# A gated H3 layer with its gradients on one core: VectorE dependence delay in the FFT stage's order, key halves loaded before the weights, D taps before the shift taps

## The chip, the cores and the metric

The kernel runs on one core of one Trainium2 chip. The metric is device time in microseconds (us) of one execution; before the change the median of six runs is 519.81 us (518.73 to 521.49). Engines are named as the profile names them: PE is the matmul engine (PEld its weight loads), DVE is VectorE, ACT is ScalarE, POOL is GpSimd, SP is SyncE, which issues DMAs.

## The reference

The forward function, with S = 2048 rows, D = 512 channels, F = 1376 and everything in bf16, is

```python
xn = layernorm(q)                                   # no scale, no offset
k_shift = sum over t of k shifted by t rows * shift_k[:, t]     # 4 taps
kv = k_shift * v
y = irfft(rfft(kv, 2S) * rfft(ssm_k, 2S))[:S] + kv * ssm_D      # along S
s = xn * y
h = sigmoid(xn @ w_gate) * (xn @ w_up)
g = silu(h @ w_down)
out = q + s * g
```

The kernel returns `out` and, for a given `grad_out`, the gradients with respect to q, k, v, shift_k, ssm_k, ssm_D, w_gate, w_up and w_down (ten outputs).

## The kernel before

**Stages.** The work has three stages on the same core. The FFT stage (to about 148 us) computes the long convolution with FFTs written as matmuls, and beside it the gate/up products of nine of the 16 row tiles (`f_gen`). The middle stage (`stepB`, to about 343 us) does the gate's output product, its gradient and the row gradient, tile by tile. The last stage runs the convolution backwards (`frontC`, `backC`) beside the weight gradients (`dW`).

**The FFT stage.** Channels go in four groups of 128 (`cg` 0 to 3). Four generators give the work; `run_streams` interleaves them:

- `strK` transforms the kernel taps of a group: `k_t` adds the D tap to tap 0 on DVE and transposes on PE, `step1` multiplies by the cosine and sine table `Cf`, `flip` transposes, `step3` multiplies by a block-diagonal matrix. Each result is stored (`KK_d`, POOL's queue), and its halves are swapped into a second tile `Ks` by two DMAs on SP's queue.
- `strV` forms k_shift * v for a group on DVE: four multiplies by a tap row of `skb`, three adds, and a multiply by v, each 128x2048. `step1` follows.
- `strX` does `flip` and `step3` for that product, multiplies it by the two tap tiles on DVE (the second product needs `Ks`), and returns through `inv3` and `inv1`.
- `f_gen` has 32, 32 and 24 128x128 matmuls for one row tile (parts 0, 1 and 2, `pi`), a sigmoid on ACT and a multiply on DVE for each; `f_ln` is the row tile's layer norm on DVE and POOL, `f_xt` its transposes.

Every PE result lies in PSUM and is copied out ("evicted") by `evac`, which may run on either ACT or DVE.

**What sets the order.** Instructions aren't issued as they are written. `Rec` records all of them with their dependences, and `Rec.order` (a greedy list scheduler) gives each engine one fixed list. It keeps a clock for each engine (`free`) and an estimate of when each operation's inputs are there (`ready`), and always takes the operation that can start first. Two of its rules are touched here. Between `late` and `early` (operation numbers) a dependent operation on the same DVE or ACT is counted as ready at its predecessor's end plus 0.034 us and a ready one within 0.125 us may be taken in front of it; outside of these numbers it is counted as ready as soon as the engine is free. `late` was set at the end of the FFT stage (operation 2406), `early` at the start of the last (5157). The other rule is the choice between ACT and DVE for an eviction: an eviction of a bf16 result (a transpose) has `bias` 0.3, and DVE takes it as if it were ready 0.3 us sooner.

An engine runs its list strictly in this order; a DMA queue's issues too. The DMAs of the start are written in this order: on ACT's queue the shift taps `skr` and the D taps `Dcol_b`; on SP's queue the SSM taps of group 0 (`ld_KT`), two row tiles, the first 512 columns of both gate weights (`ld_w(0, 512)`), the key and value columns of group 0 (`ld_k(0)` with its two halo pieces, `ld_v(0)`), a row tile, and the other weights. A key or value group is 512 KB in pieces of 256 bytes. The shift taps are spread over the partitions by four 1-row matmuls, whose results ACT copies into `skb`.

Of the kernel before, what the change touches and what calls it, by code (L numbers as in the profile page):

```python
# [16 lines left out]
P = 128  # L17
# [25 lines left out]
class Arena:  # L43


    def __init__(self, slab, nbytes):
        self.slab = slab
        self.holes = [(0, nbytes)]
# [44 lines left out]
class Ring:  # L93
# [9 lines left out]
    def next(self):  # L103
        a = self.aps[self.i % len(self.aps)]
        self.i += 1
        return a
# [64 lines left out]
class Rec:  # L171
# [8 lines left out]
    def __init__(self, nc, tc, slab, psum):  # L180
        self.nc, self.tc, self.psum = nc, tc, psum
        self.slab_name = slab.name
        self.ops = []
        self.lastw, self.readers = {}, {}
        self.late, self.early = 1 << 30, 1 << 30
        self.cache = {}
        for e in self.ENGS:
            setattr(self, e, EngRec(self, e))
# [161 lines left out]
    def order(self):  # L350
# [21 lines left out]
        free = {e: 0.0 for e in self.ENGS}  # L372
        soon = {e: [] for e in self.ENGS}
        now = {e: [] for e in self.ENGS}
        either = []
# [30 lines left out]
        while ndone < len(ops):  # L406
            best = None
            for e in self.ENGS:
                near = 0.125 if e in ("vector", "scalar") and self.late <= lo < self.early else 0.0
                while soon[e] and soon[e][0][0] <= free[e] + near:  # L410
                    heapq.heappush(now[e], heapq.heappop(soon[e])[1])
                c = None
                if now[e]:
                    n0 = now[e][0]
                    if near and ops[n0].ready > free[e]:
                        n0 = min((n for n in now[e] if ops[n].ready <= free[e] and n < n0 + 60), default=n0)
                    c = (max(free[e], ops[n0].ready) if near else free[e], n0, e, 0)
                elif soon[e]:
                    c = (soon[e][0][0], soon[e][0][1], e, 0)
                if either and e in ("scalar", "vector"):  # L420
                    o = min(either, key=lambda o: (max(o.ready, free[e]) - (o.bias if e == "vector" else 0.0), o.n))
                    s = (max(o.ready, free[e]), o.n, e, 1)
                    late = free["scalar"] - s[0] + o.bias
                    if e == "scalar" or late > (0.4 if c is None or c[0] > s[0] + 0.6 else 1.6):
                        if c is None or s[:2] < c[:2]:
                            c = s
                if c is not None and (best is None or c[:2] < best[:2]):
                    best = c
            if best is None:
                raise RuntimeError("the order is stuck: " + str({k: len(v) for k, v in blocked.items()}))  # L430
            t, n, e, shared = best
# [24 lines left out]
            d = 0.0  # L456
            if op.dma:
                occ, d = self.dcost(alt)
                me, other = ("gpsimd", "hw") if e == "gpsimd" else ("hw", "gpsimd")
                t = max(t, pipe[me] - 12.0)  # L460
# [20 lines left out]
            while held and held[0] <= lo + LOOK:  # L481
                o = ops[heapq.heappop(held)]
# [15 lines left out]
            for s in op.succ:  # L498
                if s < 0:
                    o = ops[~s]  # L500
# [4 lines left out]
                o = ops[s]  # L505
# [131 lines left out]
def kernel_impl(ctx, tc, A_q, A_k, A_v, A_shift_k, A_ssm_k, A_ssm_D, B_x, B_w_gate, B_w_up, B_w_down,  # L637
                grad_out, out_0, out_1, out_2, out_3, out_4, out_5, out_6, out_7, out_8, out_9):
    nc = tc.nc
# [21 lines left out]
    def ps_acc(shape, dt=f32, name=None):  # L661
        return nc.ps("acc", shape, dt)
# [8 lines left out]
    skb = Ring(ar, [4, D]).ap  # L671
    Dcol_b = Ring(ar, [NG]).ap
# [29 lines left out]
    def f_ln(i, part=None):  # L702
        xj = T[i]["xq"]
        if part == 1:
            f_ln2(i)
            return
        st = T[i]["st"] = lnst.next()
        nc.vector.bn_stats(st[:, 0:6], xj)
        nc.vector.bn_aggr(st[:, 6:8], st[:, 0:6])
        nc.vector.tensor_scalar_add(st[:, 8:9], st[:, 7:8], LN_EPS)  # L710
        nc.gpsimd.tensor_tensor(out=rstd_all[:, i:i + 1], in0=st[:, 8:9], in1=neghalf, op=ALU.pow)
        if part is None:
            f_ln2(i)

    def f_ln2(i):
        xj, st = T[i]["xq"], T[i]["st"]
        if PS["wide"]:
            nc.vector.tensor_scalar(xnA[:, i, :], xj, st[:, 6:7], rstd_all[:, i:i + 1], ALU.subtract, ALU.mult)
            return
        nc.vector.scalar_tensor_tensor(nmr_all[:, i:i + 1], st[:, 6:7], -1.0, rstd_all[:, i:i + 1], ALU.mult, ALU.mult)  # L720
        nc.scalar.activation(xnA[:, i, :], xj, ACT.Identity, bias=nmr_all[:, i:i + 1], scale=rstd_all[:, i:i + 1])

    def f_xt(i):
        if POS[i] > 3 and not 8 < POS[i] < 12:
            T[i]["xnT"] = xnT_r.next()
            nc.sync.dma_start_transpose(T[i]["xnT"], xnA[:, i, :])
            return
        pt = ps_tr([4, 128], name="ps_xnT")
        for db in range(4):
            nc.tensor.transpose(pt[:, db, :], xnA[:, i, db * 128:(db + 1) * 128], ident)  # L730
        T[i]["xnT"] = xnT_r.next()
        nc.evac(T[i]["xnT"], pt[:], 512)
# [65 lines left out]
    def ld_KT(cg):  # L798
        stA["KT", cg] = KT_r.next()
        nc.sync.dma_start(stA["KT", cg], A_ssm_k[cg * GW:(cg + 1) * GW, :])  # L800
# [5 lines left out]
    def ld_k(cp):  # L806
        c0, c1 = cp * GW, (cp + 1) * GW
        kh = kh_r.next()
        nc.gpsimd.memset(kh[0:1, 0:3, :], 0.0)
        nc.sync.dma_start(kh[:, 3:, :], kC[:, :, c0:c1])  # L810
        ld_halo(nc.sync, kh[:, 0:3, :], kHalo[:, 0:3, c0:c1])
        stA["kh", cp] = kh

    def ld_v(cp):
        vg = vg_r.next()
        nc.sync.dma_start(vg, vC[:, :, cp * GW:(cp + 1) * GW])
        stA["vg", cp] = vg
# [3 lines left out]
    skr, ones1 = skr_r.ap[0:1, :], ones_r.ap[0:1, :]  # L821
    def ld_x(i):
        T[i]["xq"] = xq_r.next()
        nc.sync.dma_start(T[i]["xq"], qC[:, i, :])
    nc.scalar.dma_start(skr, A_shift_k.rearrange("(o d) t -> o (d t)", o=1))
    nc.scalar.dma_start(Dcol_b, A_ssm_D.rearrange("(cg p) -> p cg", p=P))
    ld_KT(0)
    ld_x(SEQ[0])
    ld_x(SEQ[1])

    def ld_w(f0, f1):
        for w, src in ((wg, B_w_gate), (wu, B_w_up)):
            nc.sync.dma_start(w[:, :, f0:f1], src[:, f0:f1].rearrange("(db p) f -> p db f", p=P))
    ld_w(0, 512)
    ld_k(0)
    ld_v(0)
    ld_x(SEQ[2])
    ld_w(512, 1024)
    ld_w(1024, F)
# [22 lines left out]
        pass  # L862
    next(consts)
    f_ln(SEQ[0])
    next(consts)
    f_xt(SEQ[0])
    f_ln(SEQ[1])
    next(consts)
    for db in range(4):
        pb = ps_acc([512])  # L870
        nc.tensor.matmul(pb[:], ones1, skr[:, db * 512:(db + 1) * 512], start=True, stop=True)
        nc.scalar.copy(skb[:, :, db * 128:(db + 1) * 128], pb[:].rearrange("p (d t) -> p t d", t=4))
    ld_KT(1)
    ld_k(1)
    ld_v(1)
# [197 lines left out]
    for r in (KT_r, KC_r, kh_r, vg_r, acc_r, term_r, kvt_r, QgK_r, QgV_r, QfK_r, QfV_r, KF_r, Ks_r, Bg_r, Xc_r, P1_r, Ci_r):  # L1073
        r.free()
    PS["mm"], PS["wide"] = "mm1", False
    nc.late = len(nc.ops)


    zw = {k: Ring(ar, [D], at=kv_off["kh"] + 1024 * q) for q, k in enumerate(("sigz", "gate", "s_out", "dgate", "t2"))}
# [404 lines left out]
@with_exitstack  # L1484
def kernel(
    ctx: ExitStack,
    tc: tile.TileContext,
    A_q: bass.AP,
    A_k: bass.AP,
    A_v: bass.AP,  # L1490
    A_shift_k: bass.AP,
    A_ssm_k: bass.AP,
    A_ssm_D: bass.AP,
    B_x: bass.AP,
    B_w_gate: bass.AP,
    B_w_up: bass.AP,
    B_w_down: bass.AP,
    grad_out: bass.AP,
    out_0: bass.AP,
    out_1: bass.AP,  # L1500
    out_2: bass.AP,
    out_3: bass.AP,
    out_4: bass.AP,
    out_5: bass.AP,
    out_6: bass.AP,
    out_7: bass.AP,
    out_8: bass.AP,
    out_9: bass.AP,
):
    kernel_impl(tc, A_q, A_k, A_v, A_shift_k, A_ssm_k, A_ssm_D, B_x, B_w_gate, B_w_up, B_w_down,  # L1510
                grad_out, out_0, out_1, out_2, out_3, out_4, out_5, out_6, out_7, out_8, out_9)
# [30 lines left out]
```

## Time and profile before

| | us |
| --- | --- |
| median of six runs | 519.81 |
| the profiled execution | 518.73 |
| its span | 516.9 |
| PE busy | 490.1 |
| DVE busy | 390.5 |
| ACT busy | 351.2 |
| POOL busy | 126.4 |

Lines such as "L522" stand for one helper through which every operation is issued, so line numbers don't tell operations apart; shapes and places in time do. In answers about a window, "(x)" behind a busy time is the number of instructions. In a timeline the columns are start, duration, engine, operation, output and inputs, number, and the idle time in front with what ended it. The busy time of an operation can overlap the one behind it on the same engine, since an engine starts the next before the last one has ended. "ACTq" and "SPq" are the issues of DMAs on these engines.

### The profile page before, as it was taken

How to read it: one execution, taken by the hardware profiler on the slowest of the kernel's cores; microseconds unless marked ns; L12 is line 12 of the kernel's file. 1: busy time of each engine (PE TensorE's matmuls, PEld its weight loads, DVE VectorE, ACT ScalarE, POOL GpSimd, SP SyncE). 2: the span in 40 equal slices, each digit the busy share in tenths (PEclk: the TensorE clock that was granted, in tenths of full speed). 3: DMA queues.
4: the chain of work that ended last, by engine and by line, in shares of the span. 5: the costliest groups of instructions: out<-in, count | busy, mean ns of one | idle time of the engine just before them, and what ended most of it. 6: DMA issues, size and time to landing. Idle time of an engine off the chain costs nothing.

```text
span 516.9 us, 13489 instructions
## 1 busy us (share of the span) xinstructions
PE 490.1 (95%) x5381; PEld 350.7 (68%) x5437; DVE 390.5 (76%) x771; ACT 351.2 (68%) x468; POOL 126.4 (24%) x243
## 2 busy tenths in 40 slices
PE   4899898899999999999999999999999999999997
PEld 3788697798986676666666556644676755775744
DVE  8789999777848789867779988427658678883754
ACT  7799999889974564465545546426879968776621
POOL 7344433455503423414153311000000000000000
PEclk9999999999999999999999999999999999999999
DMA  8999985689999555737399947899798699999984
GB/s 223 296 291 316 294 271 180 216 248 257 233 201 228 154 162 155 216 105 192 119 250 241 267 148 179 209 277 234 168 268 222 188 264 221 244 206 254 202 224 120
DMA packets 181705, 112.93 MB, mean 218 GB/s; under 512 B 131433, under 2 KB 166153, under 8 KB 181386
## 3 DMA queue, kind: packets, MB, share of 16 engines
q1 hardware_dynamic: 170008, 78.17, 62.9%
q0 software_dynamic: 11104, 33.89, 20.4%
q8 instruction: 42, 0.69, 0.5%
q14 instruction: 21, 0.17, 0.1%
q10 hardware_dynamic: 530, 0.01, 0.1%
HBM read 37.65 MB, written 45.72 MB: 161 GB/s over the span
## 4 chain that ended last, share of the span: by engine, by line
PE 73%; ACT 10%; DVE 7%; issue 4%; DMA 3%; POOL 2%; SPq 0%; ACTq 0%; DVEq 0%; POOLq 0%
PE psum L522 73%; ACT slab L522 10%; DVE slab L522 7%; DMA out_dram<-slab 1%; POOL slab L522 1%; DMA slab<-in_A_ssm_D_dram 1%; DMA slab<-in_grad_out_dram 0%; POOL hF_d L522 0%; POOL KK_d L522 0%; SPq L522 0%; ACTq L522 0%; POOL out_dram L522 0%; POOL sF_d L522 0%; DVEq L522 0%; POOLq L522 0%
## 5 line engine op out<-in xcount | busy, mean ns | idle before, releaser
L522 PE MATMUL psum<-slab 128*128 128x128 bf16 (+5 forms) x5381 | 490.1, 253 | 23.6 <-ACT slab L522 11.1
L522 PEld LDWEIGHTS <-slab 128*128 128x128 bf16 (+2 forms) x5437 | 350.7, 99 | 162.7 <-issue 19.1
L522 DVE TENSOR_TENSOR slab<-slab 128x512 bf16<-128x512 bf16 (+6 forms) x488 | 268.6, 600 | 50.1 <-ACT slab L522 34.3
L522 ACT CAST slab<-psum 128x1024 bf16<-128x1024 f32 (+5 forms) x272 | 219.5, 852 | 93.2 <-PE psum L522 76.8
L522 ACT ACTIVATE slab<-psum 128x512 bf16<-128x512 f32 (+2 forms) x80 | 54.0, 679 | 39.3 <-PE psum L522 36.0
L522 ACT ACTIVATE slab<-slab 128x512 bf16<-128x512 bf16 (+3 forms) x71 | 56.8, 810 | 15.0 <-DVE slab L522 14.1
L522 ACT COPY slab<-psum 128x1024 bf16<-128x1024 bf16 (+1 forms) x43 | 38.3, 936 | 13.8 <-PE psum L522 13.6
L522 POOL DMA_DIRECT2D out_dram<-slab x32 | 17.5, 547 | 93.9 <-DVE slab L522 93.9
L522 DVE TENSOR_TENSOR slab<-psum,slab 128x512 bf16<-128x512 f32 (+2 forms) x47 | 29.3, 626 | 14.3 <-ACT slab L522 11.1
L522 DVE CAST slab<-psum 128x1024 bf16<-128x1024 f32 (+2 forms) x22 | 24.6, 1116 | 15.3 <-PE psum L522 13.1
L522 POOL MEMSET slab<- 1x384 bf16 (+2 forms) x13 | 4.8, 376 | 116.7 <-PE psum L522 116.4
L522 POOL DMA_DIRECT2D hF_d<-slab x48 | 26.1, 546 | 23.5 <-DVE slab L522 22.5
L522 DVE SCALAR_TENSOR_TENSOR slab<-psum,slab 128x512 bf16<-128x512 f32 x16 | 11.0, 689 | 27.1 <-PE psum L522 27.1
L522 POOL DMA_DIRECT2D KK_d<-slab x32 | 17.5, 547 | 27.3 <-ACT slab L522 20.1
L522 POOL DMA_DIRECT2D slab<-in_A_q_dram x29 | 16.1, 555 | 16.5 <-DMA out_dram<-slab 5.2
L522 DVE SCALAR_TENSOR_TENSOR slab<-slab 128x512 bf16<-128x512 bf16 (+3 forms) x41 | 17.1, 417 | 0.9
L522 DVE STREAM_TRANSPOSE slab<-slab 128x1024 f32<-128x1024 f32 x8 | 14.3, 1826 | 2.7 <-ACT slab L522 2.7
L522 DVE TENSOR_SCALAR slab<-slab 128x1 f32<-128x1 f32 (+9 forms) x48 | 12.1, 268 | 4.6 <-POOL slab L522 3.7
L522 POOL TENSOR_TENSOR slab<-slab 128x1 f32<-128x1 f32 x16 | 11.2, 701 | 16.6 <-DVE slab L522 16.4
L522 POOL DMA_DIRECT2D slab<-hF_d x18 | 9.7, 542 | 12.5 <-PE psum L522 10.1
L522 DVE BATCH_NORM_STATS2 slab<-slab 128x6 f32<-128x512 bf16 x16 | 10.9, 684 | 0.0
L522 DVE COPY slab<-psum 128x1024 bf16<-128x1024 bf16 (+1 forms) x14 | 9.0, 648 | 2.3 <-ACT slab L522 1.7
(20 smaller groups left out, 36.3 us busy)
## 6 DMA issues: line engine op xcount, KB each, us to landing
KK_d<-slab POOLq DMA_DIRECT2D x32, 256.0 KB, 4.7
slab<-KK_d SPq DMA_DIRECT2D x16, 512.0 KB, 4.5
slab<-in_A_k_dram SPq DMA_DIRECT2D x8, 512.0 KB, 8.3
hF_d<-slab POOLq DMA_DIRECT2D x32, 128.0 KB, 4.3
slab<-slab SPq DMA_DIRECT2D x32, 128.0 KB, 5.1
out_dram<-slab POOLq DMA_DIRECT2D x32, 128.0 KB, 3.0
uF_d<-slab SPq DMA_DIRECT2D x32, 128.0 KB, 2.6
gF_d<-slab SPq DMA_DIRECT2D x32, 128.0 KB, 2.8
```

Source lines behind the costliest of these rows:

```text
L522: getattr(getattr(self.nc, eng), meth)(*[place(v) for v in a], **{x: place(v) for x, v in k.items()})
```

## The change

Six edits. `late` is 0, so the dependence delay of DVE and ACT operations and the 0.125 us look-ahead also hold in the FFT stage. The bias of a bf16 eviction is now added on ACT as well as taken off on DVE, so ACT prefers another eviction that is ready within 0.3 us. `Dcol_b` is loaded in front of `skr`. Key and value of group 0 are loaded in front of the first weight columns. The four matmuls and copies that make `skb` are recorded earlier. The line that set `late` at the stage's end is gone.

```diff
@@ class Rec, __init__ @@
-        self.late, self.early = 1 << 30, 1 << 30
+        self.late, self.early = 0, 1 << 30
@@ order @@
                 if either and e in ("scalar", "vector"):
-                    o = min(either, key=lambda o: (max(o.ready, free[e]) - (o.bias if e == "vector" else 0.0), o.n))
+                    sg = 1.0 if e == "scalar" else -1.0
+                    o = min(either, key=lambda o: (max(o.ready, free[e]) + sg * o.bias, o.n))
                     s = (max(o.ready, free[e]), o.n, e, 1)
@@ kernel_impl @@
+    nc.scalar.dma_start(Dcol_b, A_ssm_D.rearrange("(cg p) -> p cg", p=P))
     nc.scalar.dma_start(skr, A_shift_k.rearrange("(o d) t -> o (d t)", o=1))
-    nc.scalar.dma_start(Dcol_b, A_ssm_D.rearrange("(cg p) -> p cg", p=P))
     ld_KT(0)
     ld_x(SEQ[0])
     ld_x(SEQ[1])
...
-    ld_w(0, 512)
     ld_k(0)
     ld_v(0)
+    ld_w(0, 512)
     ld_x(SEQ[2])
...
     f_ln(SEQ[0])
+    for db in range(4):
+        pb = ps_acc([512])
+        nc.tensor.matmul(pb[:], ones1, skr[:, db * 512:(db + 1) * 512], start=True, stop=True)
+        nc.scalar.copy(skb[:, :, db * 128:(db + 1) * 128], pb[:].rearrange("p (d t) -> p t d", t=4))
     next(consts)
     f_xt(SEQ[0])
     f_ln(SEQ[1])
     next(consts)
-    for db in range(4):
-        pb = ps_acc([512])
-        nc.tensor.matmul(pb[:], ones1, skr[:, db * 512:(db + 1) * 512], start=True, stop=True)
-        nc.scalar.copy(skb[:, :, db * 128:(db + 1) * 128], pb[:].rearrange("p (d t) -> p t d", t=4))
     ld_KT(1)
...
-    nc.late = len(nc.ops)
```

## The prediction

> **What bounds the kernel now.** I read the busy tenths first, then busy time by stretches, then what PE waited for, then single timelines. Columns of the stretches: PE, PEld, DVE, ACT, POOL busy, granted clock, DMA share, GB/s.
>
> ```profile
> PE   4899898899999999999999999999999999999997
> DVE  8789999777848789867779988427658678883754
> ACT  7799999889974564465545546426879968776621
> ...
> 0.00:22.00 22.00, 13.08 (x118) 10.58 (x119) 18.79 (x62) 17.45 (x24) 10.64 (x27) 1.00 0.99 262
> 22.00:36.00 14.00, 13.15 (x205) 11.94 (x205) 10.56 (x14) 11.71 (x16) 7.69 (x15) 1.00 0.94 263
> 36.00:50.00 14.00, 12.48 (x201) 11.45 (x200) 13.79 (x18) 13.85 (x17) 5.18 (x10) 1.00 1.06 333
> 50.00:64.00 14.00, 12.08 (x169) 10.07 (x168) 13.90 (x22) 13.77 (x17) 6.66 (x13) 1.00 0.99 284
> 64.00:78.00 14.00, 13.46 (x221) 12.51 (x219) 13.25 (x18) 13.31 (x17) 4.39 (x8) 1.00 0.89 277
> 78.00:94.00 16.00, 12.87 (x179) 10.63 (x179) 14.43 (x21) 16.00 (x19) 6.38 (x11) 1.00 0.43 143
> 94.00:148.50 54.50, 53.47 (x857) 49.77 (x865) 38.58 (x67) 47.85 (x60) 25.62 (x49) 1.00 0.97 253
> 148.50:300.00 151.50, 150.77 (x1510) 102.64 (x1523) 123.87 (x331) 82.00 (x139) 53.83 (x101) 1.00 0.72 187
> ```
>
> Before 22 us everything is start-up. From 36 to 94 us ACT never rests (56.93 of 58), DVE almost never, and PE loses 7.1. From 94 us on PE is full: it loses 1.0 to 148.5 and 0.7 to 300. So PE idle before 94 us is what there is to win: 8.0 in 22 to 94 (14.00 - 13.15 and so on), 8.9 at the start.
>
> ```profile
> PE psum L522 <- ACT slab L522: 5.6, 17, 0.5
> PE psum L522 <- DVE slab L522: 3.6, 5, 1.5
> ```
>
> PE's waits from 20 to 100 us: ACT's evictions, seventeen times, none over 0.5, so a rate and no single wait.
>
> Both kernels' instruction lists, side by side, bound the change in time. PE's are the same from its 1,948th weight load (148.5 us), and so are DVE's, ACT's, POOL's and SP's from 142 to 147 us. As PE is full from there, a shift at 148.5 us goes through to the end, and nothing else can change.
>
> **The change part by part**
>
> **Dependent DVE operations.**
>
> ```profile
> 2.30 0.43 DVE L522 TENSOR_SCALAR slab<-slab 128x512 int32<-128x512 int32 x1
> 2.76 0.69 DVE L522 SCALAR_TENSOR_TENSOR slab<-slab 128x512 int32<-128x512 int32 x1
> 3.37 0.69 DVE L522 TENSOR_TENSOR slab<-slab 128x512 int32<-128x512 int32 x1
> 4.09 0.43 DVE L522 TENSOR_SCALAR slab<-slab 128x512 int32<-128x512 int32 x1
> ```
>
> The second reads the first and starts 0.03 after its end; the third is independent and starts 0.08 before the second ends. A neighbouring dependent pair costs 0.117. In the FFT stage such pairs fall from 58 to 36: 22 x 0.117 = 2.6 of DVE. 17 of the 22 lie before 16 us, in the making of the tables, and I count them at nothing: after the second table multiply DVE now comes 0.5 early to the D taps' add and waits for that load (which landed at 5.9; 0.5 sooner by its earlier place on ACT's queue), and each of the first two layer norms now waits for POOL's power (0.68 and 1.01) with too little in between, some 0.5 and 0.8. So the last table's sine stays near 16.1. The other five give 0.6 on DVE, beside ACT: nothing.
>
> The Trainium skill, VectorE: DVE Perf Modes, section Rules for kernel authors, speaks against this part: for chained operations the drain happens regardless, so count operations. By that the reordering would give 0 instead of 2.6 of DVE time. The rows above show 0.117 between the two kinds, so I go by the rows; it doesn't alter the sum, which uses neither.
>
> **Evictions (bias and delay together).** Durations from 20 to 100 us:
>
> ```profile
> L522 ACT CAST slab<-psum 128x1024 bf16<-128x1024 f32 x47 | 46.2, 1102 | 3.5 <-PE psum L522 3.2 <-issue 0.2
> L522 ACT COPY slab<-psum 128x1024 bf16<-128x1024 bf16 x24 | 24.3, 1063 | 2.1 <-PE psum L522 1.9
> L522 DVE CAST slab<-psum 128x1024 bf16<-128x1024 f32 x4 | 4.9, 1220 | 0.6 <-PE psum L522 0.6
> L522 DVE COPY slab<-psum 128x1024 bf16<-128x1024 bf16 x6 | 4.0, 684 | 0.2 <-PE psum L522 0.2
> ```
>
> Less the overlap, the steps on ACT are 0.905 for either type, on DVE 1.15 (f32) and 0.60 (bf16). In front of the last eviction of group 0's inverse transform (at 71.95), six large evictions leave ACT and three large and one small (0.5) come: 6 x 0.905 - 3 x 0.905 - 0.5 = 2.2 less. At group 1's `inv3` (90.6) it is 3.4 less, at its inverse transform (101.8) 2.2, over the whole stage 15 large and 3 small against 13 and 1: 2.8. DVE gets nine bf16 and six f32 and gives four and nine: about +0.2 in all, +1.5 by 72 us.
>
> **The start.** I followed ACT's new list with these steps. The four copies into `skb` (0.5 each, none added) come earlier, before the third sine pair, with no reader before 26 us. Group 0's tap transposes go in front of the second sine pair and ACT waits for them about 1.2; all four `step1` evictions now come before the first row tile's transposes are evicted, so that tile's first matmuls start at about 19 instead of 13.5-14.4. That is paid back: before, PE had two matmuls of the second row tile in front and stood 1.5 at 20-21.4 for a DVE eviction at 20.96; now it runs through. `flip` 0 comes off PE at about 23.2 (22.8 before), and the first Ci eviction starts on ACT at about 37.0 (36.4 before) with 1.4 more work done. Taken as 0; ends -0.7 and +1.0.
>
> **Key halves first.** The first weight columns were complete at 8.9, the 256-byte key and value packets ran from 8.2 to 14.1. Swapped, the weights are complete at about 8.9 + 5.9 = 14.8. What hides this is the late first row tile (19); without it 14.8 against 13.5, 1.3 lost. On SP's queue everything to the other weights keeps its sum. The small halo piece moves ahead of group 1's key load, whose own halo piece stood long on SP (timeline; minimum/median/maximum of such issues in ns):
>
> ```profile
> 16.23 7.88 SPq L522 DMA_DIRECT2D slab<-in_A_k_dram  x3
> ...
> L522 SPq DMA_DIRECT2D slab<-in_A_k_dram x11: 527/688/6715, 3.2 to 54.4; - x11
> ```
>
> Three key issues in 7.88: the load, its halo piece (6.715, the longest of the eleven) and only then, at 23.6, the small one. It goes out by 17 instead of 23.6 and lands (4.4 later, the median of such pieces) by 22 instead of 28. DVE's eight shift operations of group 0 (9.9, from 28.53) can then start at 26.3, behind the first tile's last product, and end near 36.7 instead of 38.4 with one gate product (0.6) among them. Group 0's four `step1` evictions, first at 40.9 on ACT, then start at about 37.9. This lengthens nothing ACT-bound, but keeps ACT fed while it has less to do: 0 by itself.
>
> The Trainium skill, DMA: Bandwidth & Descriptors, the table at its head, asks for at least 512 B per transfer for line rate, which speaks against putting 256-byte pieces first. The rows have 1 MB of them in 5.9 and 1 MB of 1024-byte weight packets in 3.9 (5.0 to 8.9). It sets which load is late, and the start hides that.
>
> **Key group 2 on SP.** In the new list this 512 KB load is issued in front of two swaps of `Ks`. A transfer behind it stood 5.36 (37.94), one behind the value load 4.64 (44.61). Swap 0 then lands near 45.6, needed at 48; swap 1 near 51.6, needed near 52. Counted 0; ends 0 and +4.6.
>
> **POOL.** Its queue issues the same DMAs (0.54 each) in another order; the power operations keep their place among loads. 0; up to 0.5 either way.
>
> **Sum.** ACT has 2.2 less in front of group 0's end and again of group 1's, 2.8 in the stage, and was the bound from 36 to 94. I take 2.4, between the two. Far ends: 0 (in-order waits take all), and 3.4 + 1.9 = 5.3, as at group 1's `inv3` PE is 34 matmuls further (x 0.056). 518.73 - 2.4 = 516.3 for the profiled execution, which is 1.1 below its median; so 517.4.
>
> **Rivals**
>
> - *More: PE is full earlier.* If ACT's 3.4 and PE's 1.9 both hold at 90 us, PE runs full from there: 3.5 to 5.3 off, 514.5 to 516.3 (median). For: PE loses 3.1 in 78-94. Against: DVE has 3 to 4 of shift work put off there and must still do it.
> - *No change: ACT waits in order.* A gate sigmoid stands eleven places earlier on ACT (from 67.3 to about 57), one of `inv3`'s evictions is on DVE behind two products. Five such waits of 0.5 (the largest ACT wait above) cost 2.4: 519.8. Against: PE is up to three PSUM slots ahead.
> - *Slower: swap 1 of `Ks` late.* If it lands after 54.2, over 2.2 after its need, the DVE product waits, behind it two more, and ACT stands at `inv3` 1. At 4.6 late the net is +2.2: 522.0. For: DMA share is 0.99 to 1.06 there. Against: margin 0.4, and POOL's stores don't grow.
> - *The delay rule changes nothing:* excluded, 22 pairs go.
>
> **How the numbers follow.** Forecast 0.45 (own range 516.3 to 518.2), more 0.17, no change 0.21, slower 0.17. 0.3% is 1.6 us, about what a measurement of this kernel can tell from no change: under 518.2 is faster, over 521.4 slower. Faster 0.45 + 0.17 = 0.62, same 0.21; slower 0.17, with the start's +1.0 on top of an ACT wait in it. The range runs from 514.6, near the far end of "more", to 521.5: some 0.04 below, 0.16 above.
>
> **What would show it.** After: DVE's shift operations of group 0 start near 26.3; PE idle in 22 to 94 falls from 8.0 to about 5.6; ACT is still full in 36 to 90 and its busy time is about 2.8 lower; the last sine of the tables stays near 16; the later stages keep their lengths. It is wrong if DVE's products of group 0 wait for swaps, if ACT waits over 1 us at once between 36 and 94, or if the start moves by more than 1.

## The result and the profile after

| | before | after |
| --- | --- | --- |
| median, us | 520.04 (38 runs, 518.56 to 523.95) | 517.54 (17 runs, 516.21 to 519.86) |
| profiled execution, its span | 518.73, 516.9 | 519.86, 518.1 |
| ACT busy | 351.2 | 348.1 |
| DVE busy | 390.5 | 389.9 |
| PE busy | 490.1 | 490.5 |

The ratio is 0.9951 (95% interval 0.9938 to 0.9964): 2.5 us faster. One thing is needed to read the profile: the profiled execution of after is the longest of its 17, that of before the second shortest of its 38, so their spans stand the wrong way round. Places inside the execution can still be compared. Lines L522 became L523, since the change adds a line above the helper.

Busy time by stretches, after; columns as in the prediction (length, then PE, PEld, DVE, ACT, POOL busy, granted clock, DMA share, GB/s):

```profile
0.00:22.00 22.00, 11.54 (x88) 8.90 (x89) 17.55 (x61) 17.23 (x24) 11.70 (x29) 1.00 1.00 265
22.00:36.00 14.00, 13.87 (x204) 12.91 (x205) 10.52 (x13) 10.23 (x14) 5.36 (x11) 1.00 0.88 222
36.00:50.00 14.00, 12.34 (x201) 11.41 (x200) 12.20 (x17) 13.79 (x17) 5.07 (x10) 1.00 1.03 305
50.00:64.00 14.00, 13.79 (x207) 12.20 (x208) 13.89 (x23) 14.00 (x19) 7.25 (x14) 1.00 0.97 292
64.00:78.00 14.00, 13.78 (x230) 13.09 (x231) 13.22 (x15) 13.71 (x17) 4.39 (x9) 1.00 1.05 305
78.00:94.00 16.00, 15.01 (x225) 13.00 (x225) 15.40 (x27) 15.05 (x20) 7.59 (x13) 1.00 0.69 226
94.00:148.50 54.50, 52.89 (x821) 48.30 (x829) 40.07 (x71) 47.96 (x59) 24.12 (x47) 1.00 0.99 231
```

PE idle from 22 to 94 us fell from 8.0 to 3.2 (14.00 - 13.87, and so on): the gain. PE idle before 22 us rose from 8.9 to 10.5: a loss. What PE waited for from 20 to 100 us (total, times, longest) says the same, 2.9 in place of 9.2:

```profile
PE psum L523 <- ACT slab L523: 2.3, 5, 0.7
PE psum L523 <- DVE slab L523: 0.6, 2, 0.4
```

Evictions from 20 to 100 us (engine, operation, count, busy and mean ns):

```profile
L523 ACT CAST slab<-psum 128x1024 bf16<-128x1024 f32 x50 | 49.0, 1103 | 1.8 <-PE psum L523 1.8
L523 ACT COPY slab<-psum 128x1024 bf16<-128x1024 bf16 x20 | 21.0, 1073 | 1.0 <-PE psum L523 1.0
L523 DVE COPY slab<-psum 128x1024 bf16<-128x1024 bf16 x10 | 6.6, 683 | 0.0
L523 DVE CAST slab<-psum 128x1024 bf16<-128x1024 f32 x2 | 2.4, 1224 | 0.7 <-PE psum L523 0.7
```

DVE took four more of the bf16 results, which cost it 0.68 each, and gave two of the f32 ones, which cost it 1.22, back to ACT: 70 of 82 are on ACT, where it was 71 of 81. What counts for the theory is their place: up to the end of group 0's inverse transform the list has 49 large ones on ACT in place of 52.

### The profile page after: what moved, and what is told of

Same layout as the page of the kernel before. It is cut to its first block, busy times and chain, and to the rows that moved or that the text cites. A ratio compares the mean times of both kernels' runs of the same rounds, so it can differ in the third digit from the quotient of the medians.

```text
span 518.1 us, 13487 instructions
## 1 busy us (share of the span) xinstructions
PE 490.5 (95%) x5377; PEld 351.7 (68%) x5437; DVE 389.9 (75%) x775; ACT 348.1 (67%) x464; POOL 125.3 (24%) x243
## 4 chain that ended last, share of the span: by engine, by line
PE 70%; ACT 12%; DVE 10%; issue 4%; DMA 4%; SPq 0%; POOL 0%; DVEq 0%; ACTq 0%; POOLq 0%
PE psum L523 70%; ACT slab L523 12%; DVE slab L523 10%; DMA out_dram<-slab 1%; DMA slab<-in_A_ssm_D_dram 1%; DMA slab<-KK_d 1%; DMA slab<-in_grad_out_dram 0%; DMA hF_d<-slab 0%; SPq L523 0%; POOL out_dram L523 0%; DVEq L523 0%; ACTq L523 0%; POOLq L523 0%
## 5 line engine op out<-in xcount | busy, mean ns | idle before, releaser
L523 PE MATMUL psum<-slab 128*128 128x128 bf16 (+3 forms) x5377 | 490.5, 254 | 23.6 <-ACT slab L523 10.0
L523 PEld LDWEIGHTS <-slab 128*128 128x128 bf16 (+1 forms) x5437 | 351.7, 99 | 162.0 <-DVE slab L523 15.7
L523 DVE TENSOR_TENSOR slab<-slab 128x512 bf16<-128x512 bf16 (+6 forms) x488 | 268.2, 600 | 53.8 <-ACT slab L523 34.4
L523 ACT CAST slab<-psum 128x1024 bf16<-128x1024 f32 (+3 forms) x275 | 222.4, 854 | 93.0 <-PE psum L523 79.7
L523 ACT ACTIVATE slab<-psum 128x512 bf16<-128x512 f32 (+2 forms) x80 | 53.8, 679 | 45.8 <-PE psum L523 42.6
L523 ACT ACTIVATE slab<-slab 128x512 bf16<-128x512 bf16 (+3 forms) x71 | 56.5, 809 | 14.7 <-DVE slab L523 14.0
L523 ACT COPY slab<-psum 128x1024 bf16<-128x1024 bf16 (+1 forms) x36 | 33.1, 948 | 11.2 <-PE psum L523 11.2
L523 POOL DMA_DIRECT2D out_dram<-slab x32 | 17.5, 547 | 93.3 <-DVE slab L523 93.3
L523 DVE TENSOR_TENSOR slab<-psum,slab 128x512 bf16<-128x512 f32 (+2 forms) x47 | 29.2, 625 | 11.0 <-ACT slab L523 8.5
L523 POOL DMA_DIRECT2D hF_d<-slab x48 | 26.1, 546 | 37.6 <-DVE slab L523 33.3
L523 POOL MEMSET slab<- 1x384 bf16 (+2 forms) x13 | 4.5, 352 | 122.5 <-PE psum L523 119.1
L523 DVE SCALAR_TENSOR_TENSOR slab<-psum,slab 128x512 bf16<-128x512 f32 x16 | 11.0, 689 | 29.2 <-PE psum L523 29.2
L523 DVE CAST slab<-psum 128x1024 bf16<-128x1024 f32 (+2 forms) x19 | 20.9, 1102 | 15.7 <-PE psum L523 13.9
L523 POOL DMA_DIRECT2D KK_d<-slab x32 | 17.6, 549 | 18.8 <-ACT slab L523 15.5
L523 POOL DMA_DIRECT2D slab<-in_A_q_dram x29 | 16.1, 556 | 15.0 <-DVE slab L523 6.2
L523 DVE SCALAR_TENSOR_TENSOR slab<-slab 128x512 bf16<-128x512 bf16 (+3 forms) x41 | 16.9, 415 | 0.7
L523 DVE STREAM_TRANSPOSE slab<-slab 128x1024 f32<-128x1024 f32 x8 | 14.3, 1829 | 2.7 <-ACT slab L523 2.7
L523 DVE TENSOR_SCALAR slab<-slab 128x1 f32<-128x1 f32 (+9 forms) x48 | 12.2, 282 | 3.9 <-POOL slab L523 3.2
L523 DVE COPY slab<-psum 128x1024 bf16<-128x1024 bf16 (+1 forms) x21 | 13.0, 634 | 2.3 <-PE psum L523 2.3
L523 POOL DMA_DIRECT2D slab<-hF_d x18 | 9.7, 543 | 11.7 <-PE psum L523 10.1
L523 POOL TENSOR_TENSOR slab<-slab 128x1 f32<-128x1 f32 x16 | 10.3, 642 | 8.5 <-DVE slab L523 8.3
L523 POOL DMA_DIRECT2D slab<-in_grad_out_dram x16 | 8.7, 542 | 9.0 <-DMA out_dram<-slab 7.6
```

The lines of the kernel that those rows point to most:

```text
L523: getattr(getattr(self.nc, eng), meth)(*[place(v) for v in a], **{x: place(v) for x, v in k.items()})
```

## The experiments

The theory to be tested is the prediction's: ACT's rate bounds 36 to 94 us, so what ACT is spared there is the gain. The rivals were that the earlier loads give it, or the order of dependent operations on DVE. A second question came from the profile: why the stage gained more than 2.4 while the start lost.

To read the stage apart from what follows I use two places that every kernel has: the eviction of group 0's first `flip` (on ACT, at 23.10 before) for the start, and one matmul of a row tile (at 151.53 before), in front of which every kernel here has done the same matmuls (and the dummies, where there are any). "Behind the start" is the second shift less the first, so less than 0 is a gain. All in us against before, from each kernel's profiled execution, for the kernels with the change's FFT stage (in `evict_act` with six evictions on another engine):

| kernel | start | at 151.5 | behind the start | ACT's wait at 137 us |
| --- | --- | --- | --- | --- |
| after | +2.68 | -2.54 | -5.22 | 0 |
| `up_first` | +1.97 | -2.82 | -4.79 | 0.9 |
| `tail_up` | +1.91 | -3.09 | -5.00 | 0.6 |
| `spare` | +1.74 | -3.49 | -5.23 | 0 |
| `warm_up_tail` | +0.29 | -4.66 | -4.95 | 0.6 |
| `spare_all` | +0.31 | -4.93 | -5.24 | 0 |
| `tail` | +1.99 | +1.47 | -0.52 | 3.5 |
| `warm` | +1.54 | +2.72 | +1.18 | 4.0 |
| `evict_act` | +1.82 | +1.04 | -0.78 | 0.6 |

**What the parts give alone.** Four kernels: the two scheduler edits, the loads with the earlier `skb`, and the change less either scheduler edit.

```diff
@@ planner_only, from before @@
-        self.late, self.early = 1 << 30, 1 << 30
+        self.late, self.early = 0, 1 << 30
...
-                    o = min(either, key=lambda o: (max(o.ready, free[e]) - (o.bias if e == "vector" else 0.0), o.n))
+                    sg = 1.0 if e == "scalar" else -1.0
+                    o = min(either, key=lambda o: (max(o.ready, free[e]) + sg * o.bias, o.n))
...
-    nc.late = len(nc.ops)
```

> The two scheduler edits alone (dependence delay from the first operation on, bias on both engines); loads, tap matmuls and their places as before. Theory A (the gain is ACT's: less work in front of it from 36 to 94 us): most of the change's gain is here, the FFT stage ends 1.5 to 3 us earlier than before, total 517.0 to 518.5. Theory B (the gain comes from the loads, since group 0's shift operations can start earlier): no gain, 519.5 to 520.5. The start differs too: with the weights early the first row tile need not wait behind four evictions, so I expect the first flip's eviction nearer to 23 than to the 25.8 of the changed kernel.

Measured: 528.58, ratio 1.0146 (1.0125 to 1.0166). Far from both expectations, and `flip` 0 is evicted at 26.11 in its profile, not nearer to 23: with the weights early the start was late all the same.

`loads_only` is the rest of the change: `Dcol_b` in front of `skr`, `ld_k(0)` and `ld_v(0)` in front of `ld_w(0, 512)`, the `skb` block earlier, with the scheduler of before.

> The load order and the earlier tap matmuls alone; the scheduler as before. Theory A: no gain, 519.3 to 520.8, and at worst the late weights cost 1.3. Theory B: the change's gain, 517 to 518. In both the shift operations of group 0 start before 28.5.

Measured: 521.76, ratio 1.0025 (1.0003 to 1.0048). Its shift operations of group 0 start at 26.31, its start is where it was (-0.01), and group 0's inverse transform ends 0.81 later. By 151.5 us this profile, the shortest of its 12 runs, is 0.64 ahead. So the early key halves move work forward, but the median gains nothing; why not is not shown.

```diff
@@ delay_only, from after @@
-                    sg = 1.0 if e == "scalar" else -1.0
-                    o = min(either, key=lambda o: (max(o.ready, free[e]) + sg * o.bias, o.n))
+                    o = min(either, key=lambda o: (max(o.ready, free[e]) - (o.bias if e == "vector" else 0.0), o.n))
@@ bias_only, from after @@
-        self.late, self.early = 0, 1 << 30
+        self.late, self.early = 1 << 30, 1 << 30
...
+    nc.late = len(nc.ops)
```

> The change without the bias on ACT. Up to the end of group 0's inverse transform its lists have 54 large evictions on ACT and 5 on DVE, where the change as a whole has 49 and 8, and the kernel before 52 and 5; dependent neighbours on DVE are as few as in the change (27, against 32 and 52). If it is the number of evictions on ACT that counts (0.905 each), it loses 4.5 to the change at that place and is at 520.5 to 523. If the order of DVE's dependent operations itself counted, it would be at 517 to 518.5. Its lists differ in the middle stage too, which can add some us, as with the two scheduler edits alone.

> The change without the delay of dependent operations in the FFT stage. To the end of group 0's inverse transform 52 large evictions on ACT and 8 on DVE, dependent neighbours 51 as before. If ACT's evictions count, it loses 2.7 to the change there: 519.3 to 521. If DVE's dependent operations count, it loses more than the one before: 520.5 or more against 517 to 518.5.

Measured: 523.2, ratio 1.0055 (1.0026 to 1.0083), and 520.21, ratio 1.0007 (0.9984 to 1.0029). With as few dependent neighbours on DVE as the change, but more evictions on ACT, the kernel is slower than before; with 51 such neighbours, but the evictions on DVE, its time is as before. These two times would fit a delay of dependent operations that counts only as far as it moves evictions, but the profiles show that the count isn't all. Behind the start `loads_only` gains 0.63, `delay_only` 0.53 and `bias_only` 3.13, while `planner_only` loses 0.36; their starts stand at -0.01, +0.83, +3.22 and +3.01. So `bias_only` isn't as before in the stage: it wins 3.1 there and has lost 3.2 at the start. And `bias_only` and `loads_only` spare ACT the same 1.7 us up to 151.5 and gain 3.1 and 0.6; what the order in each list adds isn't shown.

None of the four alone is faster than before: +1.46% and +0.25% for the two halves, -0.49% for both. The scheduler is greedy, so each of these kernels has lists of its own, and the halves don't add. `planner_only` shows it best: of its loss 3.4 stood at 151.5 us, and 4.4 more came between there and 333 us, where its lists differ from those of both kernels.

**Is it ACT's rate that bounds the stage?** After's lists with six of the large evictions in front of 72 us put back on ACT, four bf16 (`gen_ci`, `flip`, `k_t`) and two f32 (`step1`):

```diff
+ON_ACT = {926, 980, 809, 917, 1017, 1044}
...
             for op, q, *_ in seq:
+                if op.n in ON_ACT:
+                    q = 0
                 eng, meth, a, k = op.alts[q]
```

> The changed kernel's lists; six large evictions (four of transposes, two of products) that it has on DVE before 72 us are done on ACT at the same places. ACT gets 6 x 0.905 = 5.4 more, DVE 4.7 less. Theory A (ACT's rate is the bound between 36 and 94): group 0's last inverse eviction comes 3.5 to 5.4 later than in the changed kernel (71.2), and the stage ends 2.5 to 5 later: 520 to 522.5. Rival (ACT's share was no bound, the order of the work was): under 1 us later, 517.5 to 518.5.

Measured: 522.65, ratio 1.0033 (1.0016 to 1.005). Its stretches:

```profile
36.00:50.00 14.00, 10.64 (x171) 9.83 (x172) 9.18 (x14) 13.81 (x17) 4.36 (x8) 1.00 1.03 307
50.00:64.00 14.00, 13.26 (x201) 11.78 (x202) 13.43 (x20) 14.00 (x19) 7.15 (x14) 1.00 0.85 266
64.00:78.00 14.00, 11.76 (x184) 10.75 (x184) 7.70 (x10) 14.00 (x18) 3.53 (x7) 1.00 0.96 290
```

ACT stands at 14.00 of 14, DVE has room (7.70), and PE loses 2.2 in 64 to 78 where after loses 0.2. Six steps of 0.905 are 5.4; the table shows 4.4 lost against after behind the start, the ratios 4.3. With the lists otherwise as after's, the rival's loss of under 1 is excluded: up to 78 us ACT's rate is the bound of this order.

**What the start costs.** I had taken it as 0; it is +1.7 to +2.7. Weight loads (PEld) counted in windows of two us, before, and after:

```profile
14.40:16.40 2.00, 2.00 (x20) 2.00 (x20) 1.97 (x8) 1.58 (x3) 0.00 (x0) 1.00 1.05 328
21.50:23.50 2.00, 2.00 (x37) 2.00 (x38) 0.73 (x2) 0.40 (x1) 1.24 (x4) 1.00 1.22 256
```

```profile
19.20:21.20 2.00, 2.00 (x20) 2.00 (x20) 0.86 (x4) 1.82 (x3) 1.23 (x3) 1.00 1.10 343
24.40:26.40 2.00, 2.00 (x39) 2.00 (x37) 0.76 (x2) 1.22 (x2) 0.01 (x1) 1.00 0.72 192
```

PE is "busy" in all four, with 20 loads in one kind of window and 37 or 38 in the other: 107 ns apart against 56. PE runs at half rate until it has worked for some time. Before, that time was over at 18.4, in the first row tile (a stop of 1.5 us, from 20.0 to 21.4, didn't bring the half rate back); after, PE was still at half rate when it stopped, stood from 16.2 to 19.1, and the half rate lasted to 24.3. To test it, eight dummy matmuls fill the gap:

```diff
@@ emit, in front of the first row tile's first matmul @@
+                if op.n == self.first:
+                    d, l, r = self.dummy
+                    for _ in range(8):
+                        self.nc.tensor.matmul(place(d), l, r, start=True, stop=True)
```

> The kernel after the change, with eight 128x512 dummy matmuls (nothing of the computation is left out, some is added) on PE in front of the first row tile's first matmul, into the PSUM tile that this matmul then overwrites. After the change PE idled from 15.9 to 19.1 us and then loaded weights every 107 ns until 24.1, where the kernel before was at 56 ns from 18.2 on. Theory A: it is PE's low rate that costs the start (all of it after the idling); PE is busy with the dummies from about 16 to 19.3, the 64 matmuls of the first row tile then run at 56 ns apiece and are done about 3 us sooner, flip 0 is evicted near 23 in place of 25.78, and the stage's end comes 2 to 2.7 sooner. Where the shift goes through: 514.9 to 515.5. Theory B: as A, but what the stage gains is lost at the waits for the up weights (164 us) and at the last transfers: 516.8 to 517.6, with the stage's end sooner all the same. Theory C: the start is bound by something else (ACT's list): flip 0 stays at 25.8 and the time at 517.5.

Measured: 515.8 (514.14 to 521.22), ratio 0.9929 (0.9905 to 0.9952). Its profiled execution was its longest and still at half rate to 21.3; `warm_up_tail` below, with the same dummies, shows the effect whole. Six of them in the timeline of `warm_up_tail` (start, duration), and its window of two us from 19.2:

```profile
16.95 2.09 PE L555 MATMUL psum<-slab 128*128 128x512 bf16 x6 [0.22 <-issue]
```

```profile
19.20:21.20 2.00, 2.00 (x37) 2.00 (x37) 0.91 (x4) 1.97 (x3) 1.23 (x3) 1.00 1.13 344
```

`warm_up_tail` has 37 loads in these two us, its `flip` 0 is evicted at 23.39 and its start is +0.29, so 1.4 to 2.4 us better than without the dummies. The median of `warm` is 1.7 below after's (1.1 by the ratios, whose intervals overlap; eight of its twelve runs are shorter than the shortest of after's). The dummies don't win the whole in every execution: in the profile of `warm` itself the start is +1.54.

**Where the rest goes: three suspects.** In after, x_gen's first matmul, which reads the transposed up weights, waits:

```profile
164.15 4.04 PE L523 MATMUL psum<-slab 128*128 128x512 bf16 x18 [1.92 <-DVE slab L523]
```

There the shift falls from -2.54 to -0.47. `up_first` issues the four up loads in front of the gate's last two:

```diff
@@ emit, on the finished order; behind: the gate's last two loads, up: the up weights' last @@
+        back = [s for s in seq if s[0].n in self.behind]
+        out = []
+        for s in seq:
+            if s[0].n not in self.behind:
+                out.append(s)
+            if s[0].n == self.up:
+                out += back
```

> The changed kernel; only the last two transposed loads of the gate weights go on SP's queue behind the four of the up weights. In the changed kernel's profile PE waits 1.92 at 164 us in front of the first row gradient, whose first half reads the up weights. Theory: it waits for these loads, which did not move earlier with the stage; then here the row gradient starts at about 162 and the total is 1 to 2 us below the changed kernel, 515.6 to 516.5. Rival (the wait is DVE's gradient product, as the profile's column has it): same wait, 517.5. Second rival (the gate loads are then the late ones): the wait moves 2.3 us further on and the total is 517 to 517.5.

Measured: 517.94, ratio 0.9952 (0.9937 to 0.9968), as after. Its profile loses 1.4 at another place, between 151.5 and 157 (PE waits for DVE, which waits for a tile of `grad_out`), and nothing at the row gradient. But `spare` and `tail` below, without this edit, lose nothing there either: the wait at 164 us doesn't come in every execution, so that these loads cause it isn't shown.

At the end, DVE's last six products wait for a 3-row piece, in after

```profile
503.35 7.52 DVE L523 TENSOR_TENSOR slab<-slab 128x2048 bf16<-128x2048 bf16 x6 [6.23 <-DMA slab<-slab]
```

since it is issued behind four stores that stand 4.60 on SP's queue. `tail` issues it next to its twin, and the last large store in front of two small ones:

```diff
@@ emit, on the finished order; halo: the two pieces, dk: the last large store, back: the two small ones @@
+        for s in seq:
+            n = s[0].n
+            if n not in back and n != self.halo[1]:
+                out.append(s)
+            if n == self.halo[0]:
+                out.append(pick[self.halo[1]])
+            if n == self.dk:
+                out += [pick[m] for m in back]
```

> The kernel after the change; on SP's queue the second of the last two 3-row pieces (dks of group 3) is issued right behind the first, in place of behind four stores (4.60 us), and the last 1 MB store (the key's gradient) in front of two of the last weight gradient stores. In the profile after, DVE's last six products (7.52) wait 6.23 us for this piece and the span ends 7.3 us behind them, 4.0 behind the last matmul; before the change it was 3.2. Theory A: the end is set by these products; they start some 4 sooner, the store is out before the last matmul, and the end follows PE by about 2.7 to 3: 0.8 to 1.3 off, 516.2 to 516.8. Theory B: the end is set by PE or by the DMA engines' load (share 1.0 from 420 to 500), whose bytes are the same: 517.3 to 517.8.

> As the one before, with the gate's last two transposed loads behind the four of the up weights as well, so that the stage's gain isn't lost at 164 us. With these loads alone the time was 517.94, although PE kept 1.4 us until 512 us. Theory A (the last products and their transfer set the end): now PE's 1.0 to 1.2 is passed on: 514.8 to 515.8. Theory B: nothing of it shows at the end: 517.3 to 518.

Measured: 517.77, ratio 0.996 (0.9931 to 0.9989), and 517.22, ratio 0.9941 (0.9914 to 0.9968). In `tail` the wait is shorter, and the median shows no gain:

```profile
502.89 7.52 DVE L539 TENSOR_TENSOR slab<-slab 128x2048 bf16<-128x2048 bf16 x6 [3.46 <-DMA slab<-slab]
```

The profiles do show something at the end: it comes 3.2 us behind the last matmul in all four kernels with this edit, and 3.7 to 5.1 behind it in the five others of the table (3.9 in after). The medians, of runs that spread over 1.5 to 7 us, don't resolve that.

> The three edits together: dummy matmuls at the start, the up weights' transposed loads first, the last pieces side by side. If the three losses (2 to 2.7 at the start, 1.0 to 1.9 at 164 us, 0.8 to 1.3 at the end) are separate, the sum is 3.8 to 5.9 off the time after the change: 511.6 to 513.7. If a later wait takes the start's gain, it stays at the value of the two edits without the dummies.

Measured: 515.23 (513.81 to 516.41), ratio 0.9916 (0.9891 to 0.994), above the sum that I had expected: of the three edits only the dummies move the median by more than 0.1%. Nothing of the computation is left out, and it is below both kernels.

The third suspect came out of `tail` and `warm`, whose profiled executions were among their longest. Waits of ACT from 100 to 150 us in `tail`:

```profile
ACT slab L539 <- PE psum L539: 6.8, 11, 1.5
ACT slab L539 <- DMA KK_d<-slab: 3.5, 1, 3.5
```

In its timeline, SP's transposed loads, the store on POOL's queue, and the eviction that waits for it:

```profile
129.84 13.21 SPq L539 DMA_TRANSPOSE slab<-in_B_w_down_dram  x3
...
130.66 0.54 POOL L539 DMA_DIRECT2D KK_d<-slab  x1 [0.29 <-ACT slab L539]
...
139.82 1.01 ACT L539 CAST slab<-psum 128x1024 bf16<-128x1024 f32 x1 [3.49 <-DMA KK_d<-slab]
```

`strX` has three buffers for the transformed tile; the fourth of group 3 waits until the first has been stored, 9.1 us after its issue, beside transposed loads. In seven of the table's executions this wait is 0 to 0.9, in `tail` 3.5 and in `warm` 4.0. From 26 to 138 us these two keep their distance to after, -0.7 and -1.1 (the start); at 146 us they are at +4.0 and +5.3. So the whole difference, 4.7 and 6.4, arises here, and it is more than ACT's wait. PE stands still meanwhile, for 2.9 and 3.4, and then falls back to the half rate. A stretch of `tail`, and the same one of after:

```profile
142.30:145.70 3.40, 3.40 (x35) 3.40 (x34) 1.26 (x4) 1.93 (x3) 0.55 (x1) 0.50 1.05 278
```

```profile
142.30:145.70 3.40, 3.40 (x53) 3.04 (x52) 0.42 (x1) 1.96 (x3) 0.26 (x1) 1.00 1.07 180
```

The granted clock is 0.50 in `tail`, and in `warm` it is 0.50 from 140.7 to 147.5.

`spare` gives that tile another buffer. It lies on two row tiles of q that had been loaded for `out`, so `out` isn't computed in these rows; the instructions and lists are the same.

```diff
+                    if cg == 3 and qq == 3:
+                        nc.spare = (len(nc.ops), Xc, ar.view(158720, [1024], bf16))
...
+            if v is self.spare[1] and op.n >= self.spare[0]:
+                v = self.spare[2]
```

> The kernel after the change with the same lists on every engine; the last transformed tile of group 3 (written by ACT at 137 us) gets a buffer of its own in place of the one whose store to memory was issued at 131 us. In six profiled executions of kernels with the changed stage ACT waited 0, 0.6, 0.6, 0.9, 3.5 and 4.0 us for this store to land (5.5 to 9.7 us after its issue, beside the transposed loads of the down weights). Theory A: this wait takes 0 to 4 of the stage's gain, another amount in each execution, and is a reason that the time after the change lies anywhere from 516.2 to 519.9: without it the median falls by 0.5 to 1.6, to 516 to 517, and nothing lies above 518.5. Theory B: the stage's end is held by the next thing in any case: 517.3 to 517.8, and the same spread.

> The same buffer, with the dummy matmuls at the start (they add work, nothing is left out), the up weights' transposed loads first, and the last pieces side by side. The three without the buffer gave 515.23 (0.9916 of before). Theory A: 0.5 to 1.6 less, 513.6 to 514.7. Theory B: 515 to 515.5.

Measured: 517.13 (516.52 to 518.42), ratio 0.9935 (0.9912 to 0.9958), and 514.29 (514.02 to 515.51), ratio 0.9883 (0.986 to 0.9906). The wait is gone from the profile, and the shift, -3.49, holds to 405 us. Waits of ACT in `spare` from 100 to 150 us, the only line:

```profile
ACT slab L526 <- PE psum L526: 6.7, 14, 1.1
```

Both medians are below those without the buffer, by 0.4 and 0.9, and the ranges are narrower (six runs each), but the intervals overlap: that the wait costs when it comes is shown by the two profiles, how often it comes is not.

## Why the prediction was right, and where it was not

The time was forecast at 517.4 and is 517.54. Two steps in it were wrong by about the same, with opposite signs, so that it agrees to 0.14 is luck; the mechanism in the stage is right.

- *ACT's rate bounds 36 to 94 us, PE is full behind:* right in the main. ACT's busy time fell by 3.1 (2.8 forecast), and six evictions put back on ACT cost the stage 4.4.
- *Dependent DVE operations, 0:* right. The last sine is at 15.93 (16.1 forecast), DVE's busy time in the whole fell by 0.6, and `delay_only`, with as few dependent neighbours, is no faster than before, though with more evictions on ACT.
- *The start, "taken as 0; ends -0.7 and +1.0":* wrong, and outside its ends. The first row tile did start at 19 (19.14), but `flip` 0 was evicted 1.7 to 2.7 later, where the forecast had it off PE 0.4 later. The failed piece is the rate: from 19 to 23.2 there is room for the tile's 64 matmuls and the 8 of `flip` only at 56 ns apiece; from 19.14 to 24.2 they lay 107 apart, some 48 of them, which is 48 x 0.051 = 2.4 more. With the dummies `flip` 0 is 0.3 later (`warm_up_tail`), as the forecast would have it. The trace of before showed both rates, and I didn't ask which one PE has at that place. The text itself named a start moved by more than 1 as a sign against it.
- *The sum, 2.4 "between the two":* too small. Behind the start the stage gained 4.8 to 5.2 in every execution of after's lists without a long store wait, which is near the far end, 5.3 (ACT's 3.4 and PE's 1.9), and so the rival "more". That it is made up of these two terms isn't shown: `bias_only` gained 3.1 with half of after's saving on ACT (1.7 of 3.2 up to 151.5 us), `loads_only` 0.6 with the same. What spoke against it was DVE's put-off shift work; it was done with PE losing 1.0 in 78 to 94 in place of 3.1. The start then took 1.7 to 2.7 of it back: 5.2 - 2.7 = 2.5 in after's profile.
- *Key halves first:* the mechanism is right. The small piece goes out at 15.86 in place of 23.59, and with an unmoved start (`loads_only`) the shift operations begin at 26.31, as forecast (26.3); after has 27.69, by the start, and ends them at 38.06 (36.7 forecast).
- *Key group 2 on SP, 0:* right. Swap 0 is issued at 40.62, swap 1 at 43.68 (it stands 3.54), and PE waited 0.6 for DVE in all; the slower rival, a late swap, didn't come.
- *A shift at 148.5 goes through:* in the main right (-3.49 stays -3.50 at 405 us in `spare`), but not in each execution: after's profile lost 2.1 at 164 us and 0.9 more by 507. Nor does PE's list in common bound what may happen in front of 148.5: the store wait at 137 us, with PE's half rate behind it, was in none of the rivals.

## What to carry to other kernels

A forecast can be right as the sum of two errors, so look at the terms at their own places (here: the start, the bound stage, the seam behind it) before the mechanism is believed. When work is moved later at the start of a kernel, price PE at its half rate; when work is moved in front of it, see whether PE has something to do meanwhile. A wait that stops PE for some 3 us can cost more than itself. Of an edit in several parts of a greedy scheduler, no part has a price of its own: count the operations on the bound engine in the lists that come out, and measure those lists, since equal counts gave different times here.

## What was not expected of the hardware

At the start, before and after, PE's half rate shows only in the distance between its instructions: the granted clock reads 1.00 in the windows at 14.4 and 19.2 us, where the loads lie 107 ns apart. Where PE had been at full rate already, the column does show it, as 0.50 (`tail`, 142.3 to 145.7; `planner_only`, 14.4 to 24.4). From the restart at 19.1 to 19.3 us the half rate lasted 5.1 (after), 3.3 (`up_first`), 3.8 (`tail`) and 3.1 us (`tail_up`) in executions with the same instructions in front, so the start's cost varies by 1 us (2 us more at half rate) from one execution to the next. Half rate came back behind a stop of PE of 2.9 (`tail`) and 3.4 us (`warm`), and not behind one of 1.5 (before, at 20.0) or 1.9 (after, at 162). The Trainium skill, TensorE: Matmul & The Clock Gate, Part 1 (and there "Wait — 56ns, not 53.3ns?"), states 106.7 and 55.6 ns for these two rates and a free-running activity window of about 3.4 us. The two rates fit; the half rate behind the store wait lasted 3.4 and 6.8 us, about one and two such windows, and 3.1 to 5.1 at the start, which this case doesn't explain further.

A 256 KB store to memory landed 5.7 us or less after its issue in one execution (after), and 9.1 and 9.7 us in two others (`tail`, `warm`), beside the same transposed loads. A wait that is 0 in one profile can be 4 in the next.
